# Sparse attention and a two-layer MLP: turning the sink probabilities on VectorE and through DMAs instead of on TensorE

## The chip, the cores and the metric

The kernel runs on one core of one Trainium2 chip. The metric is the device time of one launch in microseconds, 689.39 as the median of 3 runs of the kernel before (688.77 to 689.85). The trace is of one profiled execution of it.

## The reference

```
scores = (q @ k.T) / 8                     # 4 x 8 heads, 768 positions, depth 64
keep   = (key < 4) | (0 <= query - key < 128)
a      = softmax(where(keep, scores, -1e9))
x      = concat over heads of (a @ v)      # 3072 tokens x 512
h      = x @ w_in                          # 512 -> 2048
out    = max(0.01 * h, h) @ w_out          # 2048 -> 512
```

Each query sees the four first keys (the sinks) and a window of 128 keys that ends at itself. So a tile of 128 queries needs two blocks of 128 keys, the block before its own and its own, and the four sinks. All inputs are float32; the MLP weights come as 64-bit words.

## The kernel before

**Units and pairs.** The work is cut into 8 units of 384 queries (a batch half each), a unit into 4 pairs of heads, and a head into 3 tiles of 128 queries. Units 0 and 1 ("native") are computed in a plain form, units 2 to 7 ("late") in a packed one. The MLP of a unit has 16 steps `fc`, one for each 128 of the 2048 hidden columns: 12 matmuls `h<-xh/xl,wih/wil` of 384 columns (L607), ScalarE's 0.01h and VectorE's maximum (L628), a rounded half `gh` on ScalarE (L629), the rest `gl` on GpSimd (L630), and one step later 9 matmuls `o<-woh/wol,gh/gl` of 512 columns (L656). Every float32 operand is split into such a rounded part and a rest; three products replace one.

**What sets the order.** TensorE's order is written by hand. `attention_stream` is a generator that stops after each step (a tile's scores, a turn, a pair's values); `mlp_stream` is another. The loop at the end lets the attention run ahead: `LEAD0` and `LEAD` say by how many steps the attention is ahead of the MLP when the MLP of unit 0, or of a later unit, begins, and `due` spreads the rest evenly. So the attention of unit u+1 runs during the MLP of unit u. While unit 0 is in its MLP, the 32 weight blocks are decoded as well, three VectorE operations each (L189, L191, L193). The other engines' orders come from the scheduler of the framework, which places every instruction by a simulated time.

**A late pair.** For each head (`attend`): the two halves of q and k (`split_head`: ScalarE L278, GpSimd L279, L281); three tiles, each with two score matmuls (L318), a select that folds the two key blocks into 128 columns (L538), the masked minimum (L325) and the exponential (L327); then the scaling by the reciprocal of the sums (L545 to L547) and the copies of the sinks' probabilities to `sk` on GpSimd (L550, L553). Then:

- `turn_blocks` (L365): VectorE turns 32 by 32 blocks, one DMA writes them to DRAM (`kd<-kt`, L368) and four read them back to `pt` in turned order (`pt<-kd`, L370);
- `turn_sinks` (L375, L378): TensorE turns the sinks of the pair into PSUM, and VectorE copies them with a mask to `st`;
- `mask_blocks` (L390): two VectorE products with the triangles `low` and `upp` spread `pt` to the two key blocks;
- `values` (L425, L429): one matmul with `st` and 12 with `pt`, which make the pair's 384 columns of x.

`later(lag, f)` puts f off by so many tiles: the turns by `LAGT`, the masks by `LAGM`, the values by `LAGP` tiles after the pair's last tile.

Of the kernel before, what the change touches and what calls it, by code (L numbers as in the profile page):

```python
# [14 lines left out]
ALU = mybir.AluOpType  # L15
# [26 lines left out]
MASKED = 1.0e38  # L42
DEEP = 9.0e8
NATU = 2
LEAD = 10
LEAD0 = 3
LAGT = 2
LAGG = 3
LAGV = 4
LAGP = 5  # L50
LAGM = 3
PRE = 2
PRE0 = 4
# [58 lines left out]
    return lim  # L112


def late_masks(tc, cpool, tpool, masks, after):
    nc = tc.nc
    m0, m1, m2 = masks
    prv, snk, cur = slice(0, P), slice(P, W1), slice(W1, W3)
# [21 lines left out]
    pm = [m0]  # L140
    for i, m in enumerate((m1, m2)):
        pk = cpool.tile([P, W1], F32, name=f"pm{i}")
        nc.gpsimd.tensor_copy(out=pk[:, 0:NSK], in_=m[:, snk])
        with tc.issue_after(after.ins):
            nc.vector.tensor_tensor(out=pk[:, NSK:], in0=m[:, prv], in1=m[:, cur], op=ALU.max)
        pm.append(pk)
    return pm, tri, low, upp, own


@with_exitstack  # L150
def fast_path(ctx, tc, cpool, qp, qk, vu, vs, vx, vt, wq, out, ident, lims, wz, negm, wmin, wmax):
# [14 lines left out]
    wts, whole, fetched = {}, {}, {}  # L166
    anchor = [None]
    raws, vraws, svs = {}, {}, {}
    sks, late, checks, whole_lim = [], [], [], []

# [174 lines left out]
    def turn_native(u, pair, j, w, state):  # L345
# [13 lines left out]
        copy(out=state["pt"][:, :, o0:o0 + m], in_=tp[:, 0:2 * m].rearrange("p (o q) -> p o q", o=2))  # L359
        if u and j == T - 1:  # L360
            split_sinks(u, pair)

    def turn_blocks(u, pair, o, w, state):
        kt = xpool.tile([P, TU], F32, tag="rb", name=f"kt{u}_{pair}_{o}", bufs=1)
        nc.vector.transpose(kt.rearrange("p (b j x) -> p b j x", b=NSQ, x=SQ),  # L365
                            w[:, :, NSK:].rearrange("p j (b x) -> p b j x", b=NSQ))
        far = dpool.tile([P, NSQ, T * SQ], F32, tag="kt", name=f"kd{u}_{pair}_{o}", bufs=2)
        nc.sync.dma_start(out=far.rearrange("p b x -> p (b x)"), in_=kt)  # L368
        for b in range(NSQ):
            nc.sync.dma_start(out=state["pt"][b * SQ:(b + 1) * SQ, o, 0:TU].rearrange("c (a x) -> c a x", a=NSQ),  # L370
                              in_=far[:, b].rearrange("(a c) x -> c a x", a=NSQ))

    def turn_sinks(u, pair, state):
        tp = turn_bank(u, f"t{u}_{pair}")
        nc.tensor.transpose(out=tp[:, 0:P], in_=state["sk"].rearrange("p r j h s -> p (r j h s)"), identity=ident)  # L375
        st = xpool.tile([P, P + TU], F32R, tag="r", name=f"st{u}_{pair}")[:, 0:TU]
        state["st"] = st
        nc.vector.tensor_tensor(out=st.rearrange("p (j q) -> p j q", j=T),  # L378
                                in0=tp[:, 0:P].rearrange("p (o q) -> p o q", o=1).broadcast_to([P, T, P]),
                                in1=late[0][4].rearrange("p (j o) -> p j o", o=1).broadcast_to([P, T, P]),  # L380
                                op=ALU.mult)

    def mask_blocks(u, o, state):
        j0 = 1 - u % 2
        n = T - j0
        cur, prv = (state["pt"][:, o, i * TU:(i + 1) * TU].rearrange("p (a j x) -> p a j x", a=NSQ, j=T)[:, :, j0:]
                    for i in range(2))
        for dst, mask in ((prv, late[0][2]), (cur, late[0][3])):
            with tc.issue_after(anchor[0].ins):
                nc.vector.tensor_tensor(out=dst, in0=cur, in1=mask.rearrange("p (a o x) -> p a o x", a=NSQ, o=1)  # L390
                                        .broadcast_to([P, NSQ, n, SQ]), op=ALU.mult)

    def masked_keys(state, o, j0, n):
        cur = state["pt"][:, o]
        first = (j0 * SQ, TU + SQ) if j0 >= 0 else (TU, 0)
        return bass.AP(cur.tensor, cur.offset + first[0],
                       [cur.ap[0], [first[1], n], [T * SQ, NSQ], [1, SQ]])
# [21 lines left out]
    def values(u, pair, state):  # L419
# [7 lines left out]
        for kb, (po, qo, m) in enumerate(parts):  # L427
            for o in range(2):
                nc.tensor.matmul(acc[o * D:(o + 1) * D, qo:qo + m],  # L429
                                 lhsT=vv[:, kb * P + o * D:kb * P + (o + 1) * D],  # L430
                                 rhs=masked_keys(state, o, qo // P - (0 if kb or not half else 1), m // P)
                                 if packed else state["pt"][:, o, po:po + m], start=kb == 0 and not packed,
                                 stop=packed and kb == len(parts) - 1, skip_group_check=True)
        for j in range(1 - half, 0 if packed else T):
            js = slice(j * P, (j + 1) * P)
# [20 lines left out]
    def attend(u, pair, pend):  # L456
# [19 lines left out]

        def tile_pt():
            if "pt" not in state:
                state["pt"] = apool.tile([P, 2, 2 * TU], F32, tag="pt", name=f"pt{u}_{pair}", bufs=1)

        def pt_then(f, *args):
            tile_pt()
# [2 lines left out]
        if native(u):  # L485
            state["sm"] = apool.tile([P, T, 2], F32, tag="sm", name=f"sm{u}_{pair}")
            sp = raws.pop((u, pair))
            for j in range(T):
# [15 lines left out]
                if j == 0:  # L504
# [6 lines left out]
                        rest(anchor[0])  # L511
                    if u == 1 and pair == 1:
                        whole_lim.append(whole_limits(tc, cpool, lim_raw, lim_lo, anchor[0]))
                        late.append(late_masks(tc, cpool, iopool, masks, anchor[0]))
                count[0] += 1
                if j == T - 1:
                    if u == 0 and pair == 0:
# [5 lines left out]
        else:  # L523
            for o in range(2):
# [7 lines left out]
                    load_sinks(u, pair, w[:, T * W1:])  # L532
                w = w[:, 0:T * W1].rearrange("p (j k) -> p j k", j=T)
                sm = apool.tile([P, T], F32, tag="sm", name=f"sm{u}_{h}")
                for j in range(T):
                    ps, = scores(u, pair, j, (o,), sp)
                    if KSL[u % 2][j][1] == W3:
                        nc.vector.copy_predicated(out=ps[:, W1:W3], mask=late[0][1], data=ps[:, 0:P])  # L538
                        src = ps[:, P:W3]
                    else:  # L540
                        src = ps[:, 0:W1]
                    soft(u, h, j, w[:, j], src, late[0][0][min(T * (u % 2) + j, 2)], sm[:, j:j + 1])
                    count[0] += 1
# [380 lines left out]
```

## Time and profile before

| | |
|---|---|
| median of 3 runs | 689.39 us |
| profiled execution | 687.77 us, its span 686.0 us |
| TensorE matmul busy (PE) | 672.1 us, 98% of the span |
| VectorE (DVE) | 491.1 us, 72% |
| GpSimd (POOL) | 331.5 us, 48% |
| ScalarE (ACT) | 306.5 us, 45% |
| mean granted TensorE clock | 0.995 |

The span runs from the first to the last instruction; 1.8 us of the profiled execution lie outside it. PE is the stream of matmuls, PEld the loading of their weights beside it. Matmuls overlap in their pipeline, so what one costs is read from the distance of two starts and not from its own duration. Between 140 and 680 us PE is never idle.

### The profile page before, as it was taken

What the parts mean: (1) busy time and instruction counts of PE and PEld (TensorE: products, weight loads), DVE (VectorE), ACT (ScalarE), POOL (GpSimd) and SP (SyncE); (2) the same over time, 40 slices, a digit from 0 to 9 for tenths busy, and PEclk for the clock granted to TensorE, in tenths of its full rate; (3) what the DMA queues carried; (4) which work ended last, traced back from release to release, by engine and by line L of the source; (5) the groups of instructions that cost most, each with busy time, mean ns of one, the idle gap of its engine ahead of it and who ended that gap; (6) DMA issues with size and microseconds to landing.
All of it is one profiled execution on the core that took longest, in us unless ns stands there. A gap on an engine that the chain in (4) does not pass through costs nothing.

```text
span 686.0 us, 11736 instructions
## 1 busy us (share of the span) xinstructions
PE 672.1 (98%) x3794; PEld 583.4 (85%) x3794; DVE 491.1 (72%) x1240; ACT 306.5 (45%) x812; POOL 331.5 (48%) x436
## 2 busy tenths in 40 slices
PE   9999999799999999999999999999999999999996
PEld 5578888698888988888898888889888888889995
DVE  5799999677667766675777776677567766477772
ACT  5867665344444444444444444444444443222221
POOL 4667698544544554544554455445445444212221
PEclk9999999999999999999999999999999999999999
DMA  6657767343234323333333432343333442168751
GB/s 228 217 173 234 208 216 220 112 136 111 82 110 140 100 86 110 97 120 116 95 108 105 142 106 74 107 133 107 88 116 110 128 126 67 36 217 281 248 190 49
DMA packets 65216, 93.43 MB, mean 136 GB/s; under 512 B 32000, under 2 KB 44032, under 8 KB 65152
## 3 DMA queue, kind: packets, MB, share of 16 engines
q1 hardware_dynamic: 65008, 92.52, 43.5%
q8 instruction: 31, 0.51, 0.3%
q14 instruction: 33, 0.27, 0.1%
q10 hardware_dynamic: 144, 0.13, 0.1%
HBM read 76.89 MB, written 15.73 MB: 135 GB/s over the span
## 4 chain that ended last, share of the span: by engine, by line
PE 81%; DVE 0%; issue 0%
PE h L607 36%; PE o L656 35%; PE acc L429 5%; PE s L318 5%; PE acc L425 1%; PE t L375 0%; DVE ob L666 0%; PE flag_t L733 0%
## 5 line engine op out<-in xcount | busy, mean ns | idle before, releaser
L630 POOL TENSOR_TENSOR gl<-g,gh 128x384 fp32r<-128x384 f32 x121 | 138.2, 1142 | 149.2 <-ACT gh L629 149.2
L607 PE MATMUL h<-xh,wih 128*128 128x384 f32 x512 | 180.6, 353 | 1.6 <-DVE g L628 1.6
L607 PE MATMUL h<-xl,wih 128*128 128x384 f32 x512 | 173.4, 339 | 0.1
L607 PE MATMUL h<-xh,wil 128*128 128x384 f32 x512 | 173.3, 339 | 0.0
L656 PE MATMUL o<-woh,gh 128*128 128x512 f32 (+1 forms) x400 | 154.1, 387 | 0.0
L656 PE MATMUL o<-wol,gh 128*128 128x512 f32 (+1 forms) x400 | 152.9, 385 | 0.0
L327 ACT ACTIVATE pk<-pk,negm 128x132 f32<-128x132 f32 (+1 forms) x192 | 81.2, 423 | 110.5 <-DVE negm L325 106.2
L279 POOL TENSOR_TENSOR qksp<-qkraw,qksp 64x396 fp32r<-64x396 f32 (+1 forms) x48 | 56.8, 1184 | 130.3 <-issue 128.0
L656 PE MATMUL o<-woh,gl 128*128 128x512 f32 (+1 forms) x400 | 114.5, 388 | 0.3 <-POOL gl L630 0.3
L628 DVE TENSOR_TENSOR g<-h,g 128x384 f32<-128x384 f32 x127 | 70.3, 554 | 54.9 <-ACT g L621 54.4
L607 PEld LDWEIGHTS h<-xh,wih 128*128 128x128 f32 x512 | 96.6, 189 | 12.4 <-issue 6.5
L621 ACT ACTIVATE g<-h 128x384 f32<-128x384 f32 x127 | 61.7, 486 | 90.4 <-PE h L607 89.8
L607 PEld LDWEIGHTS h<-xl,wih 128*128 128x128 f32 x512 | 96.9, 189 | 1.6 <-POOL xl L444 0.4
L607 PEld LDWEIGHTS h<-xh,wil 128*128 128x128 f32 x512 | 96.6, 189 | 0.0
L656 PEld LDWEIGHTS o<-woh,gl 128*128 128x128 f32 x400 | 73.7, 188 | 16.7 <-POOL gl L630 0.7
L629 ACT CAST gh<-g 128x384 fp32r<-128x384 f32 x128 | 65.7, 514 | 43.6 <-DVE g L628 43.3
L656 PEld LDWEIGHTS o<-woh,gh 128*128 128x128 f32 x400 | 75.3, 188 | 11.2 <-issue 0.2
L656 PEld LDWEIGHTS o<-wol,gh 128*128 128x128 f32 x400 | 75.3, 188 | 10.7
L278 ACT CAST qksp<-qkraw 128x780 fp32r<-128x780 f32 (+1 forms) x48 | 43.1, 899 | 79.6 <-PE s L318 68.5
L538 DVE COPY_PREDICATED s<-tri,s 128x128 f32<-128x128 int8 x120 | 34.3, 286 | 49.2 <-PE s L318 48.9
L318 PEld LDWEIGHTS s<-qksp 128*128 128x128 f32 x288 | 53.1, 189 | 4.6
L318 PE MATMUL s<-qksp 128*128 128x260 f32 (+1 forms) x288 | 56.4, 277 | 0.0
(121 smaller groups left out, 859.5 us busy)
## 6 DMA issues: line engine op xcount, KB each, us to landing
craw<-in_wq SPq DMA_DIRECT2D x26, 512.0 KB, 4.5
qkraw<-in_qk SPq DMA_DIRECT2D x24, 454.0 KB, 3.4
qkraw<-in_qk SPq DMA_DIRECT2D x24, 390.0 KB, 3.0
kd<-kt SPq DMA_DIRECT2D x48, 192.0 KB, 2.3
pt<-kd SPq DMA_DIRECT2D x192, 48.0 KB, 2.0
wiraw<-in_wq SPq DMA_DIRECT2D x16, 512.0 KB, 3.6
woraw<-in_wq SPq DMA_DIRECT2D x16, 512.0 KB, 3.6
out<-ob SPq DMA_DIRECT2D x23, 256.0 KB, 3.5
```

Of the source, the lines that this page charges most:

```text
L278: nc.scalar.copy(out=sp[:, 0:TU + n], in_=raw[:, 0:TU + n])
L279: nc.gpsimd.tensor_tensor(out=sp[D:P, TU:TU + n], in0=raw[D:P, TU:TU + n], in1=sp[D:P, TU:TU + n].bitcast(F32), op=ALU.subtract)
L318: nc.tensor.matmul(pss[0][:, 0:kn], lhsT=sp[:, off + j * P:off + (j + 1) * P], rhs=sp[:, TU + k0:TU + k0 + kn], start=c == 0, stop=c == 1)
L327: nc.scalar.activation(out=w, in_=w, func=AF.Exp, scale=-1.0, bias=neg, accum_out=sm)
L429: nc.tensor.matmul(acc[o * D:(o + 1) * D, qo:qo + m], lhsT=vv[:, kb * P + o * D:kb * P + (o + 1) * D], rhs=masked_keys(state, o, qo // P - ...
L538: nc.vector.copy_predicated(out=ps[:, W1:W3], mask=late[0][1], data=ps[:, 0:P])
L607: nc.tensor.matmul(ph[:, 0:TU], lhsT=w[:, cs], rhs=x, start=cc == 0 and c == 0, stop=cc == NCC - 1 and c == 2)
L621: nc.scalar.mul(g, ph[:, 0:TU], 0.01)
L628: anchor[0] = nc.vector.tensor_tensor(out=g, in0=ph[:, 0:TU], in1=g, op=ALU.max)
L629: nc.scalar.copy(out=gh, in_=g)
L630: (nc.vector if u and fc == NFC - 1 else nc.gpsimd).tensor_tensor(out=gl, in0=g, in1=gh.bitcast(F32), op=ALU.subtract)
L656: nc.tensor.matmul(acc, lhsT=(gl if c == 2 else gh)[:, t * P:(t + 1) * P], rhs=(wl if c == 1 else wh)[:, cols], start=f == 0 and c == 0, s ...
```

## The change

- `turn_sinks` goes, and with it the TensorE turn. In `turn_blocks` of the pair's second head (o = 1), VectorE turns `sk` as well, as a fourth column of blocks, and the same DMAs carry it: 128 x 512 numbers to DRAM instead of 128 x 384, and back in runs of 128 numbers instead of 96. `mask_blocks` then makes `st` with one more VectorE product out of `pt`.
- `low` and `upp` are copied once into a PSUM bank (`held`), from which the masks are read; the sums of a head (`den`, `rec`) are kept there too, from the first mask on.
- `pt` becomes one buffer of 1792 columns; the joined score masks (`join_masks`) overwrite their source.
- `LAGP` is 6 instead of 5. `LEADS` is 3 for unit 0, 6 for unit 1 and 9 for the later ones, where it was 3, 10 and 10. A late unit has 28 steps instead of 32.

```diff
-LEAD = 10
-LEAD0 = 3
+LEADS = (3, 6) + (9,) * (NU - 1)
-LAGP = 5
+LAGP = 6
...
     def turn_blocks(u, pair, o, w, state):
-        kt = xpool.tile([P, TU], F32, tag="rb", name=f"kt{u}_{pair}_{o}", bufs=1)
-        nc.vector.transpose(kt.rearrange("p (b j x) -> p b j x", b=NSQ, x=SQ),
-                            w[:, :, NSK:].rearrange("p j (b x) -> p b j x", b=NSQ))
+        n, both = halves(state, o)
+        kt = xpool.tile([P, NSQ * (T + 1) * SQ], F32, tag="rb", name=f"kt{u}_{pair}_{o}", bufs=1)
+        kt = kt[:, 0:NSQ * n * SQ]
+        blk = kt.rearrange("p (b j x) -> p b j x", b=NSQ, x=SQ)
+        nc.vector.transpose(blk[:, :, 0:T], w[:, :, NSK:].rearrange("p j (b x) -> p b j x", b=NSQ))
+        if o:
+            nc.vector.transpose(blk[:, :, T], state["sk"].rearrange("p r j h s -> p r (j h s)"))
...
-    def turn_sinks(u, pair, state):
-        tp = turn_bank(u, f"t{u}_{pair}")
-        nc.tensor.transpose(out=tp[:, 0:P], in_=state["sk"].rearrange("p r j h s -> p (r j h s)"), identity=ident)
...
+    def mask_blocks(u, pair, o, state):
+        if not held:
+            held.append(bank("t", "held"))
+            for i, mask in enumerate(late[1:3]):
+                nc.scalar.copy(out=held[0][:, i * P:(i + 1) * P], in_=mask)
...
+                nc.vector.tensor_tensor(out=dst, in0=cur, in1=held[0][:, i * P:(i + 1) * P]
...
+        if o:
+            st = xpool.tile([P, P + TU], F32R, tag="r", name=f"st{u}_{pair}")[:, 0:TU]
+            state["st"] = st
+            with tc.issue_after(anchor[0].ins):
+                nc.vector.tensor_tensor(out=st.rearrange("p (j a x) -> p j a x", j=T, a=NSQ),
+                                        in0=both[:, 0, :, T:].rearrange("p a o x -> p o a x")
+                                        .broadcast_to([P, T, NSQ, SQ]),
...
-                        nc.vector.tensor_scalar(out=sm, in0=sm, scalar1=1e-9, scalar2=None, op0=ALU.add)
-                        nc.vector.reciprocal(out=sm, in_=sm)
+                        den = rec = sm
+                        if held:
+                            inv = held[0][:, 2 * P + o * 2 * T:]
+                            den, rec = inv[:, 0:T], inv[:, T:2 * T]
+                        nc.vector.tensor_scalar(out=den, in0=sm, scalar1=1e-9, scalar2=None, op0=ALU.add)
+                        nc.vector.reciprocal(out=rec, in_=den)
...
-                        if o:
-                            later(LAGT, lambda: turn_sinks(u, pair, state))
...
-    steps = [NPAIR * (2 * T + 2)] * NU
+    steps = [NPAIR * (2 * T + 2)] * NATU + [NPAIR * (2 * T + 1)] * (NU - NATU)
...
-        lead = LEAD if u else LEAD0
-        due = sum(steps[:u + 1]) + lead + (sum(steps[u + 1:u + 2]) + LEAD - lead) * (r + 1) // mlp_steps
+        lead, then = LEADS[u:u + 2]
+        due = sum(steps[:u + 1]) + lead + (sum(steps[u + 1:u + 2]) + then - lead) * (r + 1) // mlp_steps
```

Three places show what this moves. The first is TensorE's row at the last MLP step of unit 0 (`h0_15`), before:

```order
L656 MATMUL o0_2_701<-woh13_1493,gl0_13_1657 128x512
L607 MATMUL h0_15_1758<-xh0_0_296,wih15_1659 128x384
L607 MATMUL h0_15_1758<-xl0_0_297,wih15_1659 128x384
L607 MATMUL h0_15_1758<-xh0_0_296,wil15_1660 128x384
L375 MATMUL t2_0_1764<-ident_60,sk0_105 128x128
L607 MATMUL h0_15_1758<-xh0_1_403,wih15_1659 128x384
```

The same place after the change:

```order
L668 MATMUL o0_2_695<-woh13_1470,gl0_13_1594 128x512
L314 MATMUL s2_1_1_1698<-qksp2_1_1656 128x260 x2
L619 MATMUL h0_15_1704<-xh0_0_296,wih15_1596 128x384
L619 MATMUL h0_15_1704<-xl0_0_297,wih15_1596 128x384
L619 MATMUL h0_15_1704<-xh0_0_296,wil15_1597 128x384
L619 MATMUL h0_15_1704<-xh0_1_403,wih15_1596 128x384
```

The turn `t2_0` of the third unit's first pair (`sk0` holds its sinks) stood among these matmuls and is gone, and the scores that run here are of head 1 of unit 2 (`s2_1`), where before they were already of head 2.

The second place is VectorE's row between the maxima `g0_14` and `g0_15` of the last two MLP steps of unit 0, before:

```order
L628 TENSOR_TENSOR g0_14_1736<-h0_14_1699,g0_14_1736 128x384
L325 ISA pk2_2_1722,negm_65<-s2_2_1_1746,pm0_675 128x132
L325 ISA negm_65 128x1
L390 TENSOR_TENSOR pt2_0_1676<-pt2_0_1676,low_660 128x4x64
L547 TENSOR_TENSOR pk2_1_1595<-pk2_1_1595,sm2_1_1599 128x396
L390 TENSOR_TENSOR pt2_0_1676<-pt2_0_1676,upp_661 128x4x64
L365 STREAM_TRANSPOSE kt2_0_1_1706<-pk2_1_1595 128x384
L378 TENSOR_TENSOR st2_0_1766<-t2_0_1764,own_669 128x384
L538 COPY_PREDICATED s2_2_2_1784<-tri_662,s2_2_2_1784 128x128
L628 TENSOR_TENSOR g0_15_1777<-h0_15_1758,g0_15_1777 128x384
```

After the change:

```order
L640 TENSOR_TENSOR g0_14_1649<-h0_14_1627,g0_14_1649 128x384
L370 STREAM_TRANSPOSE kt2_0_0_1725<-pk2_0_1426 128x384
L450 TENSOR_TENSOR r1_3_1636<-acc1_3_1672,r1_3_1636 128x384
L267 TENSOR_TENSOR sv2_1_1869<-pk2_2_1770,sv2_1_1869 32x128
L548 COPY_PREDICATED s2_1_1_1698<-tri_662,s2_1_1_1698 128x128
L321 ISA pk2_1_1662,negm_65<-s2_1_1_1698,m1_97 128x132
L321 ISA negm_65 128x1
L548 COPY_PREDICATED s2_1_2_1733<-tri_662,s2_1_2_1733 128x128
L640 TENSOR_TENSOR g0_15_1717<-h0_15_1704,g0_15_1717 128x384
```

The first masks of the third unit (on `pt2_0`) and the scaling of its second head (`pk2_1`) have moved behind `g0_15`. What has come in is the end of the last native pair (`r1_3`) and the turn of the first late head (`kt2_0_0`).

The third place is the queue of DMAs that SP issues, at pair 1 of unit 4. Before:

```order
L368 DMA kd4_1_0_3715<-kt4_1_0_3713 128x384
L238 DMA v4_2_3532<-in_vu0 128x384
L370 DMA pt4_1_3712<-kd4_1_0_3715 32x4x96 x4
L248 DMA qkraw5_0_4081<-in_qk1 128x908
L368 DMA kd4_1_1_3753<-kt4_1_1_3751 128x384
L370 DMA pt4_1_3712<-kd4_1_1_3753 32x4x96 x4
```

After:

```order
L374 DMA kd4_1_0_3687<-kt4_1_0_3685 128x384
L244 DMA qkraw5_0_4069<-in_qk1 128x908
L234 DMA v4_2_3531<-in_vu0 128x384
L376 DMA pt4_1_3684<-kd4_1_0_3687 32x4x96 x4
L374 DMA kd4_1_1_3751<-kt4_1_1_3748 128x512
L376 DMA pt4_1_3684<-kd4_1_1_3751 32x4x128 x4
```

The load of the values `v4_2` waits for the matmuls of the pair before (4, 0), which free its buffer, and the reading back of `pt4_1` stands behind it. The load of the next head's q and k has moved ahead of that wait, and the second trip to DRAM carries 512 columns.

## Rows read from the trace of the kernel before

**Rows 1.** Busy time by stretch: us of each engine, granted clock, DMA share
```profile
34.00:120.00 86.00, 85.33 (x500) 70.27 (x499) 81.36 (x185) 56.69 (x139) 67.72 (x84) 1.00 0.68 209
140.00:680.00 540.00, 540.00 (x3017) 480.09 (x3016) 371.64 (x932) 218.81 (x577) 234.35 (x280) 1.00 0.39 120
```
**Rows 2.** Waits of PE from 34 to 140 us: total, times, longest
```profile
PE t L375 <- POOL sk L553: 2.9, 1, 2.9
PE h L607 <- DVE g L628: 1.6, 2, 1.3
PE o L656 <- POOL gl L630: 0.3, 1, 0.3
```
**Rows 3.** Timeline of PE around 126 us: start, us, engine, line, what [idle before]
```profile
126.57 0.33 PE L375 MATMUL t<-ident,sk 128*128 128x128 f32 x1 [2.86 <-POOL sk L553]
...
127.02 0.53 PE L607 MATMUL h<-xl,wih 128*128 128x384 f32 x1
127.34 0.53 PE L607 MATMUL h<-xh,wil 128*128 128x384 f32 x1
```
**Rows 4.** Busy time by stretch, the 3.3 us after that wait (clock is third last)
```profile
126.60:129.90 3.30, 3.30 (x12) 3.30 (x13) 0.60 (x2) 0.02 (x1) 0.00 (x0) 0.52 0.24 79
```
**Rows 5.** Timeline of PE around a later turn of the sinks
```profile
311.84 0.27 PE L375 MATMUL t<-ident,sk 128*128 128x128 f32 x1
311.86 0.42 PE L607 MATMUL h<-xh,wih 128*128 128x384 f32 x1
312.12 0.34 PE L607 MATMUL h<-xl,wih 128*128 128x384 f32 x1
312.30 0.34 PE L607 MATMUL h<-xh,wil 128*128 128x384 f32 x1
```
**Rows 6.** The line of the turn: count, shortest, median and longest in ns
```profile
L375 PE MATMUL t<-ident,sk x24: 271/272/334, 126.6 to 593.2; 128*128 128x128 f32 x24
```
**Rows 7.** Groups of VectorE's instructions: count, busy us, mean ns, idle before
```profile
L547 DVE TENSOR_TENSOR pk<-pk,sm 128x396 f32<-128x396 f32 x48 | 51.1, 1064 | 0.9
L545 DVE TENSOR_SCALAR sm<-sm 128x3 f32<-128x3 f32 x48 | 32.7, 681 | 3.8 <-ACT pk L327 3.8
L390 DVE TENSOR_TENSOR pt<-pt,low 128x256 f32<-128x256 f32 (+1 forms) x48 | 29.8, 620 | 4.5 <-DMA pt<-kd 4.5
L365 DVE STREAM_TRANSPOSE kt<-pk 128x384 f32<-128x384 f32 x48 | 27.3, 568 | 0.3
L378 DVE TENSOR_TENSOR st<-t,own 128x384 fp32r<-128x384 f32 x24 | 13.3, 555 | 4.4 <-PE t L375 4.3
L442 DVE TENSOR_TENSOR r<-acc,r 128x384 f32<-128x384 f32 x8 | 4.4, 549 | 4.2 <-PE acc L436 4.2
L337 DVE TENSOR_SCALAR s<-sm 128x6 f32<-128x6 f32 x8 | 1.3, 164 | 1.0 <-ACT pk L327 0.8
```
**Rows 8.** Timeline of one late pair, from the pair before's values to its own
```profile
301.19 0.28 PE L425 MATMUL acc<-st,sv 128*128 128x256 f32 x1
...
303.56 2.17 SPq L370 DMA_DIRECT2D pt<-kd  x4
...
304.31 0.40 PE L318 MATMUL s<-qksp 128*128 128x260 f32 x2
...
306.61 0.52 ACT L629 CAST gh<-g 128x384 fp32r<-128x384 f32 x1 [0.24 <-DVE g L628]
...
309.74 0.40 PE L656 MATMUL o<-woh,gh 128*128 128x512 f32 x1
...
311.61 1.74 SPq L370 DMA_DIRECT2D pt<-kd  x4
...
317.07 0.41 DVE L390 TENSOR_TENSOR pt<-pt,upp 128x256 f32<-128x256 f32 x1
...
321.03 0.28 PE L425 MATMUL acc<-st,sv 128*128 128x256 f32 x1
```
**Rows 9.** DMA issues: count, KB each, median us to landing
```profile
kd<-kt SPq DMA_DIRECT2D x48, 192.0 KB, 2.3
pt<-kd SPq DMA_DIRECT2D x192, 48.0 KB, 2.0
```

More of the change, by code (lines that the diff above doesn't have):

```diff
@@ L112, in whole_limits, with late_masks @@
     return lim
-def late_masks(tc, cpool, tpool, masks, after):
+def late_masks(tc, cpool, tpool, after):
     nc = tc.nc
-    m0, m1, m2 = masks
-    prv, snk, cur = slice(0, P), slice(P, W1), slice(W1, W3)
     low = cpool.tile([P, P], F32, name="low")
@@ L139, in late_masks, with join_masks @@
         nc.vector.tensor_reduce(out=own, in_=rows, axis=AX.X, op=ALU.max)
[L140 to L147, printed above, removed]
+    return tri, low, upp, own
+def join_masks(tc, masks):
+    for m in masks[1:]:
+        tc.nc.vector.tensor_tensor(out=m[:, W1:W3], in0=m[:, 0:P], in1=m[:, W1:W3], op=ALU.max)
+    return [masks[0]] + [m[:, P:W3] for m in masks[1:]]
 @with_exitstack
@@ L168, in fast_path @@
     raws, vraws, svs = {}, {}, {}
-    sks, late, checks, whole_lim = [], [], [], []
+    sks, late, joined, held, checks, whole_lim = [], [], [], [], [], []
     def fetch_weights(fc):
@@ L358, in turn_native, with halves @@
         copy = nc.vector.tensor_copy if u == 0 and pair == 0 else nc.scalar.copy
-        copy(out=state["pt"][:, :, o0:o0 + m], in_=tp[:, 0:2 * m].rearrange("p (o q) -> p o q", o=2))
+        pt = state["pt"][:, 0:4 * TU].rearrange("p (o q) -> p o q", o=2)
+        copy(out=pt[:, :, o0:o0 + m], in_=tp[:, 0:2 * m].rearrange("p (o q) -> p o q", o=2))
         if u and j == T - 1:
             split_sinks(u, pair)
+    def halves(state, o):
+        n = T + o
+        both = state["pt"][:, o * 2 * TU:][:, 0:2 * NSQ * n * SQ]
+        return n, both.rearrange("p (t a j x) -> p t a j x", t=2, a=NSQ, j=n)
@@ L368, in turn_blocks @@
+        kt = kt[:, 0:NSQ * n * SQ]
[3 more added lines that the diff above has]
+            nc.vector.transpose(blk[:, :, T], state["sk"].rearrange("p r j h s -> p r (j h s)"))
+        far = dpool.tile([P, NSQ, n * SQ], F32, tag=f"kt{o}", name=f"kd{u}_{pair}_{o}", bufs=2)
         nc.sync.dma_start(out=far.rearrange("p b x -> p (b x)"), in_=kt)
         for b in range(NSQ):
-            nc.sync.dma_start(out=state["pt"][b * SQ:(b + 1) * SQ, o, 0:TU].rearrange("c (a x) -> c a x", a=NSQ),
+            nc.sync.dma_start(out=both[b * SQ:(b + 1) * SQ, 0].rearrange("c a j x -> c a (j x)"),
@@ L371, in turn_blocks @@
                               in_=far[:, b].rearrange("(a c) x -> c a x", a=NSQ))
-    def turn_sinks(u, pair, state):
-        tp = turn_bank(u, f"t{u}_{pair}")
-        nc.tensor.transpose(out=tp[:, 0:P], in_=state["sk"].rearrange("p r j h s -> p (r j h s)"), identity=ident)
[L376 to L381, printed above, removed]
@@ L383, in mask_blocks @@
-    def mask_blocks(u, o, state):
+    def mask_blocks(u, pair, o, state):
[3 more added lines that the diff above has]
+                nc.scalar.copy(out=held[0][:, i * P:(i + 1) * P], in_=mask)
+        n, both = halves(state, o)
         j0 = 1 - u % 2
[L385 to L388, printed above, removed]
+        cur, prv = both[:, 0, :, j0:T], both[:, 1, :, j0:T]
+        for i, dst in enumerate((prv, cur)):
@@ L389, in mask_blocks @@
             with tc.issue_after(anchor[0].ins):
-                nc.vector.tensor_tensor(out=dst, in0=cur, in1=mask.rearrange("p (a o x) -> p a o x", a=NSQ, o=1)
-                                        .broadcast_to([P, NSQ, n, SQ]), op=ALU.mult)
+                nc.vector.tensor_tensor(out=dst, in0=cur, in1=held[0][:, i * P:(i + 1) * P]
+                                        .rearrange("p (a o x) -> p a o x", a=NSQ, o=1)
+                                        .broadcast_to([P, NSQ, T - j0, SQ]), op=ALU.mult)
@@ new lines, in mask_blocks @@
+        if o:
[5 more added lines that the diff above has]
+                                        .broadcast_to([P, T, NSQ, SQ]),
+                                        in1=late[3].rearrange("p (j o q) -> p j o q", o=1, q=1)
+                                        .broadcast_to([P, T, NSQ, SQ]), op=ALU.mult)
@@ L393, in masked_keys @@
     def masked_keys(state, o, j0, n):
[L394 to L397, printed above, removed]
+        m, both = halves(state, o)
+        at = both[:, 0, :, j0] if j0 >= 0 else both[:, 1, :, 0]
+        return bass.AP(at.tensor, at.offset, [at.ap[0], [(NSQ * m + 1) * SQ, n], [m * SQ, NSQ], [1, SQ]])
     def gather(u, pair, state):
@@ L431, in values @@
                                  rhs=masked_keys(state, o, qo // P - (0 if kb or not half else 1), m // P)
-                                 if packed else state["pt"][:, o, po:po + m], start=kb == 0 and not packed,
+                                 if packed else state["pt"][:, o * 2 * TU + po:o * 2 * TU + po + m], start=kb == 0 and not packed,
                                  stop=packed and kb == len(parts) - 1, skip_group_check=True)
@@ L478, in tile_pt @@
             if "pt" not in state:
-                state["pt"] = apool.tile([P, 2, 2 * TU], F32, tag="pt", name=f"pt{u}_{pair}", bufs=1)
+                state["pt"] = apool.tile([P, 2 * TU + 2 * NSQ * P], F32, tag="pt", name=f"pt{u}_{pair}", bufs=1)
         def pt_then(f, *args):
@@ L513, in attend @@
                         whole_lim.append(whole_limits(tc, cpool, lim_raw, lim_lo, anchor[0]))
-                        late.append(late_masks(tc, cpool, iopool, masks, anchor[0]))
+                        late.extend(late_masks(tc, cpool, iopool, anchor[0]))
                 count[0] += 1
@@ L534, in attend @@
                 sm = apool.tile([P, T], F32, tag="sm", name=f"sm{u}_{h}")
+                if not joined:
+                    joined.extend(join_masks(tc, masks))
                 for j in range(T):
@@ L537, in attend @@
                     if KSL[u % 2][j][1] == W3:
-                        nc.vector.copy_predicated(out=ps[:, W1:W3], mask=late[0][1], data=ps[:, 0:P])
+                        nc.vector.copy_predicated(out=ps[:, W1:W3], mask=late[0], data=ps[:, 0:P])
                         src = ps[:, P:W3]
@@ L541, in attend @@
                         src = ps[:, 0:W1]
-                    soft(u, h, j, w[:, j], src, late[0][0][min(T * (u % 2) + j, 2)], sm[:, j:j + 1])
+                    soft(u, h, j, w[:, j], src, joined[min(T * (u % 2) + j, 2)], sm[:, j:j + 1])
                     count[0] += 1
                     if j == T - 1:
-                        nc.vector.tensor_scalar(out=sm, in0=sm, scalar1=1e-9, scalar2=None, op0=ALU.add)
-                        nc.vector.reciprocal(out=sm, in_=sm)
-                        nc.vector.tensor_tensor(out=w, in0=w, in1=sm.rearrange("p (j o) -> p j o", o=1)
+                        den = rec = sm
[4 more added lines that the diff above has]
+                        nc.vector.reciprocal(out=rec, in_=den)
+                        nc.vector.tensor_tensor(out=w, in0=w, in1=rec.rearrange("p (j o) -> p j o", o=1)
                                                 .broadcast_to([P, T, W1]), op=ALU.mult)
@@ L555, in attend @@
                         later(0 if o else LAGT, lambda o=o, w=w: pt_then(turn_blocks, u, pair, o, w, state), "quiet")
-                        if o:
-                            later(LAGT, lambda: turn_sinks(u, pair, state))
-                        later(LAGM if o else LAGT + LAGM, lambda o=o: mask_blocks(u, o, state), "quiet")
+                        later(LAGM if o else LAGT + LAGM, lambda o=o: mask_blocks(u, pair, o, state), "quiet")
                     yield
@@ L691, in fast_path @@
     done = 0
-    while done < steps[0] + LEAD0:
+    while done < steps[0] + LEADS[0]:
         done += 1
```

1 line of the change is left out of this document (removed).

## The prediction, made before the changed kernel ran

> **What bounds the kernel now.** I read the busy times by stretch first. From 140 to 680 us TensorE (PE) is busy for 540.00 of 540.00 us at full clock, while VectorE has 371.64 and GpSimd 234.35 [rows 1]. In that stretch only the sum of the matmuls counts: an instruction that leaves PE is gained whole, and time saved on another engine is worth nothing. Before it, from 34 to 120 us, where the weights are decoded beside the attention, PE has 85.33 of 86 us and VectorE 81.36 of 86: PE leads by little, and VectorE is nearly full. The list of PE's waits shows what goes wrong where the two meet: one wait of 2.9 us of the sinks' turn for GpSimd's copy `sk`, two waits, 1.6 us together, of `h` for VectorE's maximum `g`, and one of 0.3 us for `gl` [rows 2]. They are PE's only waits between 34 and 140 us, and from 140 on it has none. So the change can gain in two ways: turns off PE, 24 times, and the pause near 126 us.
>
> **The change part by part.**
>
> *The turns of the sinks.* There are 24 of them [rows 6]. Their 272 ns overlap with the next matmuls, so the price is read from starts: from the turn at 311.84 to the second `h` after it at 312.12 are 0.28 us, for the turn and one `h`; one `h` takes 0.18 (312.12 to 312.30). The turn costs 0.10 us, and 24 of them 2.5. The low bound is the 0.02 between the turn's start and the next (0.5 in all), the high one its whole 0.27 (6.5). I take 2.5, because the `h` behind the turn visibly starts its successor late [rows 5].
>
> The Trainium skill speaks against this step: VectorE: DVE Perf Modes, The three transpose paths, counts VectorE's transpose as one of 32 by 32 blocks only and calls a DMA that turns by strides far slower, and its rules for kernel authors give TensorE for a 128 by 128 turn. On latency the trace agrees: 0.27 us on TensorE [rows 6] against two DMA trips of 2.3 and 2.0 us [rows 9]. By the rule the move is a loss. By the rows it is one only if someone waits for those trips, which is the first rival below.
>
> *The pause near 126 us.* The turn of the third unit's first pair stands in the middle of `h0_15` and waits 2.86 us for `sk` [rows 3], which waits for the scaling of the second head on a full VectorE. That instruction is gone from PE, and the 2.9 us with it, unless something else stands there late. The 1.6 us for `g` have to come from VectorE. `LEADS` lets unit 0's MLP carry 30 + 6 - 3 = 33 attention steps where it carried 30 + 10 - 3 = 37, so VectorE's row up to `g0_15` loses the two masks (0.62 each), the scaling (1.06), the second turn of blocks (0.57) and `st` (0.56), 3.4 us by their means [rows 7], and three tiles' selects and minima besides. 3.4 is more than 1.6, so I count this wait as gone.
>
> *The clock.* Behind the pause the `h` matmuls start 0.32 us apart [rows 3] where they take 0.18 otherwise [rows 5]: the granted clock is 0.52 on the mean of the 3.3 us after the pause, that is the lower of the two levels, 1.2 GHz, nearly throughout [rows 4]. Half of it is lost, 3.3 x (1 - 0.52) = 1.6 us. PE had been idle for most of the time from the first wait for `g` on. Without the pause this goes too.
>
> *What is added on VectorE.* Per pair one turn of 128 columns: no row has it; it lies between nothing and the 0.57 of 384 columns, and I take a third and a little, 0.25. `st` reads SBUF instead of PSUM: between 0.55 (as now) and 1.06 (the scaling, two SBUF operands), taken as 0.6. What moves to PSUM gets cheaper by the nearest rows: the sum 0.16 instead of 0.68 and the scaling 0.55 instead of 1.06, twice a pair [rows 7]; the four masks lie between 0.42 (the quick one at 317.07 [rows 8]) and their mean of 0.62. Per pair that is +0.25 + 0.05 - 2 x 0.52 - 2 x 0.51 - 4 x 0.1, about 2 us less. On the path this is zero from 140 us on, since PE waits for no one there; were that cover gone, it would still be a gain. None of it reaches the first wait near 122 us, since the PSUM bank is filled only at the third unit's first mask. ScalarE's two copies into it and the joined masks are single instructions of some 0.3 us off the path.
>
> *Values a tile later, and the queues.* The sinks now come with the second trip to DRAM. Before, its reading back was issued from 311.61 to 313.35, landed 2.0 later near 315.4, and the last mask ended at 317.48; the values began at 321.03, 3.5 us later [rows 8, 9]. Pairs follow each other every 19.8 us (301.19 to 321.03), a tile every 3.3. With `LAGP` 6 the spare is 3.5 + 3.3 less `st` (0.6) and the second turn (0.25): 6 us. SP's queue gets one thing worse: the values' load waits for the pair before's values, which now come a tile later, and behind it stands the reading back of the first head. It ended its issue at 305.73, landed near 307.7, 6.5 us after the values' first matmul at 301.19. The masks of that head follow two tiles, 6.6 us, after those values instead of three. So VectorE may stand there for up to a microsecond a pair. Queued behind it are the next minimum and the next `g`. `gh` ended at 307.13 and its first `o` began at 309.74 [rows 8]: 2.6 us are free, and PE doesn't notice a wait of one.
>
> *The sum.* 2.5 + 2.9 + 1.6 + 1.6 = 8.6 us. I take 0.6 off, two waits like the 0.3 of `gl`, because unit 1's MLP now starts with less lead (6 steps instead of 10) and its last pair's `xl` is made just before. Net 8.0: 687.77 of the profiled execution becomes 679.8. The median of the runs lies 1.62 higher, so 681.4. Head (to 34 us) and tail (from 680 us) don't change.
>
> **The rivals.**
>
> *VectorE's wait for the turned blocks reaches PE (slower).* Place: the first mask of each late pair. From 2.6 us of waiting on, `g` comes too late for `o`, 24 times. If the queue of DMAs slips by one tile, VectorE waits 3.3 us, PE 0.7 a pair: 24 x 0.7 = 17, less the 8.0: 698. For: the spare there shrinks from a tile to nearly nothing, and VectorE already waits 4.5 us in all for `pt<-kd` [rows 7]. The rule on transposes above would raise this chance. Against: those 4.5 us cost PE nothing, and 2.6 us of slack are measured.
>
> *The pause moves instead of going.* PE then stands as long at the start of unit 1's MLP, for `xl` of the last native pair or for `g0_14`, and drops to half clock again. Only the turns are gained: 689.39 - 2.5 = 686.9. For: VectorE stays full up to there (81.36 of 86 [rows 1]), since the 32 decodings stay, and the lead of unit 1 shrinks. Against: four steps fewer before `g0_15`, and in the new order 21 `h` and 18 `o` stand on PE between the last native values and the use of `xl`, at 0.18 each or more, 7 us for three instructions. The Trainium skill (TensorE: Matmul & The Clock Gate, HAM oscillation) says that TensorE falls back to half rate when it idles between bursts; the trace agrees with 0.52 after the pause [rows 4].
>
> *The turns are hidden in the pipeline.* If each costs PE only 0.02, the gain is 8.0 - 2.0 = 6.0: 683.4. Against: the spacing of [rows 5].
>
> **How the numbers follow.** Forecast 0.70, its own range 679.5 to 683; hidden turns 0.08 (683.4); moved pause 0.14 (686.9); VectorE's wait 0.08 (698). A difference of 0.2%, 1.4 us, is about what a measurement of this kernel can tell from none. The lowest time is that without new waits, 689.39 - 8.6 - 0.3 (the wait for `gl` too) - 0.67 (all of PE's idle time from 34 to 120 us, which holds some of it already), some 679.5, with half a microsecond of spread 679.0. The upper end takes in the moved pause, 687.0; what is left out is mostly the wait of VectorE. All but that rival end below 688.0, and half of a moved pause with a small wait may end within 0.2%: faster 0.87, same 0.06, slower 0.07.
>
> **What would show it.** Right: no wait of PE over 0.5 us from 34 us on; the granted clock at full from 34 to 680 us; no matmul between the scores and the values that turns sinks; VectorE's busy time down by some 40 us with no effect on PE; the span near 678. The DVE group of masks should show longer idle time before it, ended by `pt<-kd`, and PE's list of waits nothing of it. Wrong: a wait of PE of over 2 us between 110 and 130 us with a stretch at half clock (the pause moved), or PE idle once a pair after 140 us (the DMA trips). If neither is there and the time still differs by over 2 us, the price of a turn was misread.

## The result, and the profile of the changed kernel

The changed kernel takes 680.2 us (median of four runs, 680.03 to 681.37) against 689.1 of the kernel before: ratio 0.9874, 95% interval 0.9857 to 0.9891. The forecast was 681.4 us, with a range of 679.0 to 687.0. Its profiled execution took 681.37 us with a span of 679.6, 6.4 less than that of before; two later profiles of the same kernel have spans of 678.9 and 678.6.

Busy time by stretch of the changed kernel, with the columns of [rows 1, 4]:
```profile
34.00:120.00 86.00, 84.01 (x488) 68.37 (x484) 79.68 (x173) 55.87 (x136) 64.37 (x81) 1.00 0.66 201
126.60:129.90 3.30, 3.30 (x21) 3.04 (x20) 2.46 (x9) 1.72 (x6) 2.68 (x3) 1.00 0.30 60
140.00:674.00 534.00, 533.89 (x2981) 474.91 (x2979) 326.27 (x960) 223.58 (x579) 220.86 (x279) 1.00 0.41 126
```
Against [rows 1, 4] the 3.3 us that ran at 0.52 of the clock are at full speed. VectorE, the third engine in each line, fell from 371.64 to 326.27 us in the late stage (which is 6 us shorter here), while PE stays full. The first stage got worse for PE: 84.01 of 86 us where it was 85.33.

The waits of PE from 34 to 140 us (total, times, longest), beside [rows 2]:
```profile
PE t L350 <- ACT pt L356: 1.1, 1, 1.1
PE o L668 <- POOL gl L642: 0.3, 1, 0.3
PE h L619 <- DVE g L640: 0.2, 1, 0.2
PE acc L437 <- ACT r L419: 0.2, 1, 0.2
```
The 2.9 us are gone, and of the 1.6 us for `g` 0.2 are left. New is a wait of a native pair's turn, at 106 us, for ScalarE's copy.

VectorE's groups, beside [rows 7] (count, busy us, mean ns, idle before):
```profile
L389 DVE TENSOR_TENSOR pt<-pt,held 128x256 f32<-128x256 f32 (+1 forms) x96 | 45.6, 475 | 1.6 <-DMA pt<-kd 0.6 <-issue 0.2
L561 DVE TENSOR_TENSOR pk<-pk,held 128x396 f32<-128x396 f32 x46 | 25.9, 564 | 0.8
L396 DVE TENSOR_TENSOR st<-pt,own 128x384 fp32r<-128x384 f32 x24 | 20.7, 864 | 7.0 <-DMA pt<-kd 6.9
L372 DVE STREAM_TRANSPOSE kt<-sk 128x128 f32<-128x128 f32 x24 | 7.4, 308 | 2.4 <-POOL sk L567 1.6
L559 DVE TENSOR_SCALAR held<-sm 128x3 f32<-128x3 f32 x46 | 7.3, 159 | 16.5 <-ACT pk L323 16.4
```
The sum fell from 681 to 159 ns, the scaling from 1064 to 564, the masks from about 604 to 475; the new turn costs 308 and `st` went from 555 to 864. Per pair that is 2 x 0.52 + 2 x 0.50 + 4 x 0.13 - 0.31 - 0.31 = 1.9 us, 24 times 46; the busy time fell by 46.6, from 491.1 to 444.5.

**A ruler for the runs.** The `h` matmuls of each MLP unit come in the same number in every version, so the starts of the first `h` of the first, third and last unit cut the span into stages that can be compared one by one, however the whole time of a run scatters. PE's timeline, of before and of the second repetition of the changed kernel, at the third and the last of these marks:
```profile
211.29 0.42 PE L607 MATMUL h<-xh,wih 128*128 128x384 f32 x1
...
610.39 0.34 PE L607 MATMUL h<-xh,wih 128*128 128x384 f32 x1
```
```profile
206.59 0.33 PE L619 MATMUL h<-xh,wih 128*128 128x384 f32 x1
...
603.33 0.34 PE L619 MATMUL h<-xh,wih 128*128 128x384 f32 x1
```
In us, with the span's rest behind the last mark (the names of runs are explained below):

| run | first mark | units 0 and 1 | units 2 to 6 | rest | span |
|---|---|---|---|---|---|
| before | 34.93 | 176.36 | 399.10 | 75.65 | 686.0 |
| changed, first | 35.66 | 171.70 | 396.74 | 75.54 | 679.6 |
| changed, third time | 34.95 | 171.64 | 396.74 | 75.30 | 678.6 |
| sched_only | 34.90 | 172.69 | 399.10 | 75.08 | 681.8 |
| old_leads | 34.82 | 178.47 | 396.73 | 75.60 | 685.6 |
| turns_back | 35.69 | 174.22 | 403.04 | 75.25 | 688.2 |
| masks_sbuf | 34.80 | 171.93 | 398.62 | 75.75 | 681.1 |
| lagm2 | 34.78 | 171.72 | 400.12 | 75.67 | 682.3 |

So the gain of 7.4 us between the spans of 686.0 and 678.6 is 4.7 in units 0 and 1 (the pause, and four of the 24 turns), 2.4 in units 2 to 6 (the other 20 turns), and 0.3 behind.

### The profile page after: what moved, and what is told of

It reads as the page before. It is cut to its first block, busy times and chain, and to the rows that moved or that the text cites. A ratio compares the mean times of both kernels' runs of the same rounds, so it can differ in the third digit from the quotient of the medians.

```text
span 679.6 us, 11735 instructions
## 1 busy us (share of the span) xinstructions
PE 667.6 (98%) x3770; PEld 579.9 (85%) x3770; DVE 444.5 (65%) x1264; ACT 311.6 (46%) x814; POOL 318.3 (47%) x434
## 4 chain that ended last, share of the span: by engine, by line
PE 89%; DVE 6%; DMA 2%; issue 1%; ACT 1%; POOL 0%; DVEq 0%; POOLq 0%; ACTq 0%
PE o L668 38%; PE h L619 37%; PE acc L437 6%; PE s L314 5%; PE s L309 1%; DMA qkn<-in_qp 1%; DVE pk L321 1%; DVE do L185 1%; PE warm L285 1%; PE t L350 1%; DVE do L187 1%; DVE wi L189 1%; DVE di L185 1%; DMA wiraw<-in_wq 1%; DMA qkraw<-in_qk 1%
## 5 line engine op out<-in xcount | busy, mean ns | idle before, releaser
L642 POOL TENSOR_TENSOR gl<-g,gh 128x384 fp32r<-128x384 f32 x121 | 125.1, 1034 | 192.5 <-ACT gh L641 184.5
L619 PE MATMUL h<-xh,wih 128*128 128x384 f32 x512 | 176.2, 344 | 0.4 <-DVE g L640 0.2
L668 PE MATMUL o<-wol,gh 128*128 128x512 f32 (+1 forms) x400 | 154.9, 390 | 0.0
L321 DVE CUSTOM_DVE_ANT_0 pk<-s,m 128x132 f32<-128x132 f32 (+1 forms) x192 | 59.8, 319 | 20.9 <-PE s L314 14.7
```

The lines of the kernel that those rows point to most:

```text
L321: anchor[0] = nc.vector.tensor_tensor_reduce(out=w, in0=src, in1=mask, scale=-SCALE, scalar=3.0e38, op0=ALU.add, op1=ALU.min, accum_out=neg)
L619: nc.tensor.matmul(ph[:, 0:TU], lhsT=w[:, cs], rhs=x, start=cc == 0 and c == 0, stop=cc == NCC - 1 and c == 2)
L642: (nc.vector if u and fc == NFC - 1 else nc.gpsimd).tensor_tensor(out=gl, in0=g, in1=gh.bitcast(F32), op=ALU.subtract)
L668: nc.tensor.matmul(acc, lhsT=(gl if c == 2 else gh)[:, t * P:(t + 1) * P], rhs=(wl if c == 1 else wh)[:, cols], start=f == 0 and c == 0, s ...
```

## The experiments

**Which part took the pause.** The theory was that the leads did, since VectorE had too much to do before unit 0's last maxima; the rival, that the pause hangs on the turn. `sched_only` is the kernel before with the leads alone, `old_leads` the changed kernel without them (the lines that matter):
```
sched_only (of before):  LEADS = (3, 6) + (10,) * (NU - 1)
                         lead, then = LEADS[u:u + 2]    # as in the change
old_leads (of the change):
-LEADS = (3, 6) + (9,) * (NU - 1)
+LEADS = (3, 10) + (9,) * (NU - 1)
```


> The kernel before with the new leads alone (3, then 6, then its own 10); the 24 turns stay on TensorE, masks, denominators and values stay as before. My theory: the pause near 126 us came from VectorE having too much to do before unit 0's last maximum, so the leads alone take it away (2.9 + 1.6 + 1.6 us, less 0.6 for new waits): 689.1 - 5.5 = 683.6 us, half clock gone. Rival: the pause hangs on the turn of the sinks on TensorE and only moves with it: 688 to 689 us, with a wait of the turn for sk of 2 us or more and a stretch at half clock somewhere else.

Measured 683.6 us, ratio 0.9929 (0.9913 to 0.9946), clock full throughout. The ruler shows 3.7 us less in units 0 and 1 and exactly the 399.10 of before in units 2 to 6. Its waits of PE from 34 to 140 us:
```profile
PE h L606 <- DVE g L627: 1.5, 2, 1.1
PE t L353 <- ACT pt L358: 0.4, 1, 0.4
PE o L655 <- POOL gl L629: 0.2, 1, 0.2
```
So the leads alone take away the turn's wait and the half clock. The reason that the theory gave isn't borne out, though: the waits for `g` are 1.5 us, as they were (1.6). Nor is `sk` ready sooner. The end of GpSimd's work on it and PE's turn, in `sched_only`:
```profile
130.31 0.21 POOL L552 TENSOR_TENSOR sk<-pk,sk 128x12 f32<-128x12 f32 x1
...
131.99 0.27 PE L374 MATMUL t<-ident,sk 128*128 128x128 f32 x1
```
In the kernel before:
```profile
126.30 0.21 POOL L553 TENSOR_TENSOR sk<-pk,sk 128x12 f32<-128x12 f32 x1
```
`sk` is done 4.0 us later than before, at 130.5, but PE asks for it 8.3 us later, at 131.99 and not at 123.71 (126.57 less the wait of 2.86). The time of 683.6 us hits the forecast, but the two profiled spans differ by 4.2 us and not by 5.5: the turn's 2.9 and the clock's 1.6 came, the 1.6 for `g` didn't.

> The changed kernel with the third unit begun four steps earlier again (leads 3, 10, then 9); all else of the change stays. My theory: the turn of the sinks is gone from TensorE and its 2.9 us stay gained, but VectorE is again behind with unit 0's last maxima g, 1.6 us of waits and some half clock behind them: 680.2 + 2 to 3 = 682 to 683 us. Rival: with the turn off TensorE there is no pause at either lead, 680.2 us, and the leads were worth nothing. Second rival: the turn was only the first to wait, another matmul stands there as long: 685 us or more.

Measured 686.7 us, ratio 0.9966 (0.9951 to 0.9982): the second rival. Its waits of PE from 34 to 140 us:
```profile
PE acc L433 <- DVE st L396: 3.8, 1, 3.8
PE h L619 <- DVE g L640: 2.1, 2, 1.8
PE o L668 <- POOL gl L642: 0.2, 1, 0.2
```
The chain of work that PE waited for there (start, us, what), PE's timeline, and the stretch behind it:
```profile
129.38 3.31 DMA kd<-kt
132.68 0.02 issue
132.70 0.34 SPq L376
...
134.05 2.07 DMA pt<-kd
...
136.57 0.48 DVE st L396
```
```profile
137.18 0.55 PE L433 MATMUL acc<-st,sv 128*128 128x256 f32 x1 [3.81 <-DVE st L396]
```
```profile
137.20:143.00 5.80, 5.80 (x22) 4.49 (x23) 2.72 (x8) 0.78 (x2) 0.42 (x2) 0.50 0.54 154
```
With the turn off PE the next instruction that needs the same sinks, the values, waits 3.8 us; PE then runs 5.8 us at half clock. What it waits for are the two trips through DRAM: the write is issued at 129.38 us and has landed at 132.68, the reading back starts 0.02 us later and has landed at 136.12. In units 2 to 6 the run equals the changed kernel. So the removed turn was where PE waited, not why.

The changed kernel has the sinks no sooner. VectorE's and PE's timelines there, in its first profile:
```profile
136.94 1.36 DVE L396 TENSOR_TENSOR st<-pt,own 128x384 fp32r<-128x384 f32 x1 [0.66 <-DMA pt<-kd]
```
```profile
142.93 0.28 PE L433 MATMUL acc<-st,sv 128*128 128x256 f32 x1
```
`st` begins at 136.94 us; in the chain of `old_leads` above it stands at 136.57. But PE comes to the values at 142.93 and not at 133.37 (137.18 less 3.81). As in `sched_only`, the leads help by letting PE ask later, not by making the sinks sooner.

**The price of a turn.** The rivals were 0.10, 0.02 and 0.27 us.
```
+            for _ in range(3 if heads[0] and j == 1 else 0):
+                nc.tensor.transpose(out=pss[0][:, 3 * P:], in_=ident, identity=ident)
```


> The changed kernel with three turns of the constant identity matrix on TensorE in each of the 24 late pairs, ahead of one score matmul, into unused columns of its bank; nobody waits for them and they wait for nothing new: 72 turns. At the 0.10 us of the prediction 7.5 us more, 687.7 us. If a turn hides in the pipeline (0.02 us): 681.6 us. If it costs its whole 0.27 us: 699.8 us.

Measured 688.4 us, ratio 0.9997 (0.9988 to 1.0006): some 8 us more than the changed kernel's 680.2, for 72 turns. By the ruler, free of the waits in unit 0, the 60 turns of units 2 to 6 cost 403.04 - 396.74 = 6.3 us, 0.105 each. PE's timeline shows the same:
```profile
398.82 0.34 PE L621 MATMUL h<-xh,wil 128*128 128x384 f32 x1
399.00 0.49 PE L313 MATMUL s<-ident 128*128 128x128 f32 x3
399.25 0.49 PE L316 MATMUL s<-qksp 128*128 128x260 f32 x2
399.57 0.39 PE L670 MATMUL o<-woh,gh 128*128 128x512 f32 x1
```
Three turns take 0.25 us to the next start, and the two scores behind them 0.32 instead of the 0.24 that they take elsewhere: 0.33 for three.

**What VectorE's saved time is worth.** Masks and denominators are read from SBUF again (parts of the edit):
```
-            held.append(bank("t", "held"))        (and the two copies into it)
+            held.append(None)
-                        in1=held[0][:, i * P:(i + 1) * P]
+                        in1=late[1 + i]
-                        if held:
+                        if held and held[0]:
```


> The changed kernel with the two masks and the denominators read from SBUF again instead of PSUM; all else of the change stays. VectorE should be busy some 25 to 45 us longer. My theory: TensorE waits for nobody after 140 us, so the time stays within 0.2% of the changed kernel's, 680.2 us. Rival: VectorE's slower instructions delay g or the masks until TensorE waits once a pair: 682 us at 0.1 us a pair, 690 us or more if a wait for the turned blocks comes with it.

Measured 682.4 us, ratio 0.9907 (0.9891 to 0.9922); VectorE is busy 507 us, 63 more, where 25 to 45 were expected. By the ruler 1.9 us are lost in units 2 to 6, so zero was wrong. TensorE waits neither for `g` nor for the turned blocks, but for a PSUM bank of the output, which VectorE has to empty. The timelines of VectorE and PE where a unit's first `o` begin:
```profile
371.04 1.36 DVE L387 TENSOR_TENSOR pt<-pt,low 128x384 f32<-128x384 f32 x1 [0.18 <-DMA pt<-kd]
372.33 1.36 DVE L394 TENSOR_TENSOR st<-pt,own 128x384 fp32r<-128x384 f32 x1
...
373.68 0.68 DVE L680 COPY ob<-o 128x512 f32<-128x512 f32 x1
```
```profile
373.72 0.40 PE L666 MATMUL o<-wol,gh 128*128 128x512 f32 x1
374.41 0.50 PE L666 MATMUL o<-woh,gh 128*128 128x512 f32 x1 [0.29 <-DVE ob L680]
374.75 0.39 PE L666 MATMUL o<-wol,gh 128*128 128x512 f32 x1
```
The copy that empties the bank stands behind a mask and `st`, 1.36 us each; the second `o` here starts 0.69 us after its forerunner instead of 0.23, and two of those behind it come 0.1 late each. It happens once a unit, five times, 0.1 to 0.7 us each time. The changed kernel has 0.23 at these places. A long `st` alone doesn't do it. VectorE at the same place of the changed kernel, third time:
```profile
370.37 1.36 DVE L396 TENSOR_TENSOR st<-pt,own 128x384 fp32r<-128x384 f32 x1 [0.20 <-DMA pt<-kd]
...
371.71 1.27 DVE L682 COPY ob<-o 128x512 f32<-128x512 f32 x2
```
`st` is as long there, but no mask stands between it and the `g` before it, and the copy is in time. So the moves to PSUM earn nothing by themselves, but without them the changed kernel loses 1.9 us. Which of the moved masks and denominators matters for that was not tried one by one.

**How near the slower rival was.** The masks and `st` one tile sooner (`LAGM = 2` for 3):

> The changed kernel with LAGM 2 instead of 3: the masks and st come one tile (3.3 us) sooner after the turned blocks were sent off. VectorE then waits for both readings back, by the first profile about 1.7 us for the first head's and 3.0 us for the second's, in every late pair, some 100 us in all. Theory: a wait up to the 2.6 us of slack between gh and its first use costs TensorE nothing and only what lies above counts, at most 0.4 us a pair: 680 to 690 us. Rival: TensorE feels the whole of a wait of VectorE through g: over 24 x 3 us more, above 740 us. Second rival: nothing is felt at all, 680.2 us.

Measured 684.3 us beside 681.2 of the changed kernel on the same chip (ratios 0.9937, 0.9922 to 0.9953, and 0.9896, 0.9882 to 0.9910). VectorE's and PE's waits after 140 us:
```profile
DVE pt L389 <- DMA pt<-kd: 54.5, 33, 3.3
```
```profile
PE o L668 <- ACT gh L641: 2.3, 3, 1.0
```
VectorE stands 54.5 us, up to 3.3 at a time, where some 100 us in all were expected, and PE loses 3.4 by the ruler, 2.8 of it at the first `o` of units 2, 4 and 6. The 33 waits are 1.7 us long on the mean, and most cost nothing, as the slack of 2.6 us said; but with a tile less the slower rival begins. The rule that gives such a turn to TensorE (the Trainium skill, VectorE: DVE Perf Modes, Rules for kernel authors) is thus outweighed here only as long as the two trips have three tiles: with two, units 2 to 6 take 400.12 us, more than the 399.10 with the turn on TensorE; with three they take 396.74.

**What is left in unit 0.** The changed kernel twice more, as yardstick for the others:

> The changed kernel again, unedited, as the yardstick of this round: 680.2 us, ratio 0.987. The wait of 1.0 us of a score matmul for its queries at 13.3 us, which its first profile shows and that of the kernel before doesn't: by my theory it belongs to that one execution, since nothing before 34 us was changed, and is gone or much shorter here (span 678.5). Rival: the change makes it, and it stands here again.

681.2 us, ratio 0.9896 (0.9882 to 0.9910), span 678.9; the wait at 13.3 us is 0.2. 

> The changed kernel once more, as the yardstick for the next three on the same chip: ratio 0.987 to 0.990, 680 to 681 us, with the wait of 1.0 us of a turn for pt near 105 us.

680.4 us, ratio 0.9870 (0.9846 to 0.9894); that wait is gone, that for `pt` is 1.2. Four edits went for the latter.
```
head_first:   load_head(...) moved ahead of load_values(...) in fetch
leads5:       LEADS = (3, 5) + (9,) * (NU - 1)
cast_later:   with tc.issue_after(turned[-2].ins) if u == NATU and h == 1 else ExitStack():
                  nc.scalar.copy(out=sp[:, 0:TU + n], in_=raw[:, 0:TU + n])
              (turned: the copies into pt, in order)
leads8:       LEADS = (3, 8) + (9,) * (NU - 1)
```


> The changed kernel with one edit: in each attention step that loads both, the next head is loaded ahead of the next pair's values, which wait for their buffer and hold up SyncE's queue behind them. Theory: the second late head then arrives before ScalarE wants it at 102.5 us, ScalarE doesn't stand 2.5 us for qkraw, the copy pt comes in time and TensorE's wait of 1.1 us at 106.4 us goes: 680.2 - 1.0 = 679.2 us. Rival: the head's own buffer isn't free any earlier either, the load starts at the same time, and nothing changes: 680.2 us.

680.7 us, 0.9885 (0.9871 to 0.9899): the wait is 1.1 again. In SyncE's queue the values' load is still issued first (98.83, the head at 99.62 us), so the edit changed nothing at that place. In `leads5` the head is first there and still starts at 99.77, after SyncE's queue waited 1.8 us for a decoding (`wo`) on VectorE. So the values ahead of it are not what holds it.

> The changed kernel with the leads 3, 5, then 9: the third unit begins one attention step later still. Theory: VectorE and ScalarE have a little more room before unit 0's last maxima, the waits of 1.1 and 0.2 us between 104 and 112 us get shorter, and unit 1's first matmuls still find xl ready: 679.3 to 680.2 us. Rival: unit 1's MLP now starts before the last native pair's values are split, TensorE waits for xl or g near 128 to 136 us: 681 us or more.

680.8 us, 0.9894 (0.9880 to 0.9908): no difference that can be told. The wait for `pt` is 0.5, but those for `gl` are 0.7.

> The changed kernel with one edit: on ScalarE the cast of the second late head, which stands ahead of the copy pt at 104 us and waits 2.4 us there for its load, though its scores come only at 118 us, is placed two copies of pt later. Theory: the copy no longer stands behind that wait, TensorE's wait of 1.0 us at 105.4 us goes, and the time falls by 0.8 to 1.0 us against the changed kernel of this round. Rival: the cast now holds ScalarE before g and gh at 107 to 108 us, and h or o waits as long there: no difference.

681.6 us, 0.9878 (0.9847 to 0.9909): no gain, the rival. Its waits of PE from 34 to 140 us:
```profile
PE h L621 <- DVE g L642: 1.8, 1, 1.8
PE acc L439 <- ACT r L421: 0.6, 1, 0.6
PE o L670 <- POOL gl L644: 0.3, 1, 0.3
PE t L352 <- ACT pt L358: 0.2, 1, 0.2
```
The wait for `pt` fell to 0.2, and 1.8 us for `g` stand 5 us later instead.

> The same edit with the leads 3, 5, then 9. Theory: the two add, since leads 5 shortened the same wait to 0.5 us and left smaller ones for gl and g: 0.8 to 1.2 us less than the changed kernel of this round, no more than 0.3 us from the run with the edit alone. Rival: the edit moves the cast into the wait for gl: no difference from the changed kernel.

680.9 us, 0.9877 (0.9853 to 0.9901): no gain either, 2.1 us for `g`.

> The changed kernel with the leads 3, 8, then 9: between the schedule of before (10, which cost 6.5 us and half clock) and the new one (6). Theory: the pause is a threshold, VectorE's debt in front of unit 0's last maxima; with two of the four steps back the waits for g come back in part and the values' wait for st doesn't: 1 to 3 us above the changed kernel of this round. Rival: the cost goes with the number of steps, half of 6.5: 3.3 us. Second rival: it only breaks at 10, no difference.

681.1 us, 0.9882 (0.9858 to 0.9906): no difference that can be told, the second rival. Its waits:
```profile
PE h L619 <- DVE g L640: 2.0, 4, 0.9
PE o L668 <- POOL gl L642: 0.3, 1, 0.3
```
In every version from 5 to 8 PE waits 1.2 to 2.9 us in unit 0, for VectorE, ScalarE or GpSimd in turn, and the clock stays full through all of these waits; at 10 there are 6 us of waits and half clock. No version tried is faster than the changed kernel by more than the runs scatter.

## Why the prediction was right, and where it wasn't

The total came out within its range, and the price of a turn and the clock came out by the mechanism that was named. The pause went for another reason than the prediction gave, so that part of the sum was luck: the change brought the leads with it.

- *A turn costs 0.10 us.* Right: 0.105. It gives 2.1 us in the 20 pairs of units 2 to 6, where 2.4 were gained; the other 0.3 are open.
- *The turn is gone from PE, and the 2.9 us with it, unless something else stands there late.* The wrong step, hidden in a right sum: something else does stand there, the values, 3.8 us in `old_leads`. The leads took the 2.9 us, as `sched_only` shows with the turns still in place, and they did it by letting PE ask for the sinks later.
- *3.4 us less on VectorE is more than 1.6, so the wait for `g` goes.* It fell to 0.2, but not for that reason: with the leads alone 1.5 us for `g` remain. In the changed kernel PE already stands 1.1 us for `pt` 5 us earlier (0.4 in `sched_only`). VectorE isn't ahead: what remains moves between `pt`, `g` and `gl` when one is relieved.
- *0.6 us for new waits.* Too little. PE's idle time from 34 to 140 us other than the 0.38 that before has too, near 37 and 42 us, is 1.6 us in the first profile. With the 0.7 us that the head took longer there (a load at 13.3 us, nearly absent in the other two profiles) this explains the 6.4 us in place of the 8.0 between the two profiled executions.
- *The clock.* Right: full until 677.7 us.
- *VectorE some 40 us less, and none of it on the path.* 46.6 less. None of it is on the path of the changed kernel. But the saved time was not without worth: `st` with two SBUF operands takes 0.86 and not 0.6 us, and with masks and denominators in SBUF too the kernel loses 1.9 us.
- *Values a tile later, a wait of up to 1 us a pair for the first head's blocks.* It stands at `st`, for the second head's, 6 times and 2.0 at most; PE notices none. The slower rival was one tile away.
- *Rivals.* The moved pause came true in small, 1.1 us and without half clock, and in unit 0 instead of at unit 1's start; by the prediction's own sign, no wait over 0.5 us, that is a miss. Hidden turns are refuted.
- *Two slips of the working.* 689.39 - 8.6 - 0.3 - 0.67 is 679.8 and not some 679.5; nothing else hangs on it. And PE was idle for most of the time only from its longer wait for `g` on, the 1.3 us, and not from the first.

What stays open is which of VectorE's and ScalarE's instructions would have to go before 124 us to end the last waits in unit 0.

## What to carry to other kernels

Where an engine waits at an instruction, ask when it asks for the data and when the data are there: taking the instruction away handed the wait to the next user of the same data here, and what removed it was an order in which that user comes later. An instruction on a full engine is priced by the starts of its neighbours and not by its duration. An engine with much idle time can still be late once a stage, where it empties a bank, so time saved there is worth nothing only as long as it isn't late.

## What the runs showed of the hardware

`st` reads the same two SBUF operands each time and takes 0.55 to 1.37 us. Two of them in the changed kernel, with GpSimd's instructions near them:
```profile
530.24 1.02 POOL L277 TENSOR_TENSOR qksp<-qkraw,qksp 128x384 fp32r<-128x384 f32 x1
530.31 1.37 DVE L396 TENSOR_TENSOR st<-pt,own 128x384 fp32r<-128x384 f32 x1 [0.19 <-DMA pt<-kd]
...
569.44 0.55 DVE L396 TENSOR_TENSOR st<-pt,own 128x384 fp32r<-128x384 f32 x1
570.20 1.02 POOL L642 TENSOR_TENSOR gl<-g,gh 128x384 fp32r<-128x384 f32 x1 [3.67 <-ACT gh L641]
```
Where a GpSimd instruction already runs, as in 20 of the 24 cases, `st` ends 0.41 to 0.45 us after it (here at 531.68 against 531.26); where none does, it takes 0.55 to 0.56, as all 24 did with an operand in PSUM. In `masks_sbuf` 20 of 24 take 1.36 to 1.37 us; there the mask ahead of it has two SBUF operands too, and takes 1.36 at 371.04 us. The Trainium skill (SBUF — State Buffer, Who interferes with whom) says that an instruction of VectorE with two SBUF inputs contends with a GpSimd instruction that reads SBUF; these rows agree, and they are why 0.6 was too low.
